# Where TensorE's operands start in a partition: one byte modulo 256 for all of them, in an attention and Fourier-mixing kernel

## The chip, the cores and the metric

The kernel runs on one core of a Trainium2 chip. The metric is the device time of one execution in microseconds (us), the median of several runs. TensorE (PE) multiplies matrices: an LDWEIGHTS loads a 128x128 stationary operand from the on-chip memory, and the MATMUL behind it streams a moving operand of up to 512 columns past it. VectorE (DVE), ScalarE (ACT) and GpSimd (POOL) work on tiles; SyncE (SP) issues most of the transfers.

## The reference, cut to what matters

Four layers on x of 2048 rows and 640 numbers, each with a residual sum and a layer norm without gains ahead of it.

```python
x = x + A(layernorm(x)); x = x + B(layernorm(x))
x = x + A(layernorm(x)); x = x + B(layernorm(x))

A: q, k, v = x @ wqkv                     # 32 heads of 20 numbers
   row s sees rows s, s-2, ..., s-14      # 8 taps, masked at the start
   o = softmax(q.k * scale) @ v;  return o @ wo
B: a = x @ dft_hid_re.T;  b = x @ dft_hid_im.T
   return dft_seq_re @ a - dft_seq_im @ b
```

## The kernel before, in words

**Products.** Every float32 number that TensorE multiplies is held as a pair, a rounded high part (float32r) and the low rest. A product is three passes, high by high, high by low, low by high (`PASSES`).

**Layer A** (`layer_a`, layers 0 and 2) is written as a list of steps, ordered by hand into phases; nothing reorders the engines' queues afterwards. The rows stand in 4 chunks c of 4 groups j of 128 rows. For each chunk, each quarter q of the weights and each j, `qkv_mm` (L366) makes one product of 15 matmuls: stationary is the transposed x of the group, in the buffer `s{j}`, moving are 480 columns of a weight row k of `wq[q]`, in the buffer `r1_{q}`. ACT empties the result (`qkv_evac`, L373), transfers put q, k and v into DRAM and fetch windows of them into the five buffers `win`. DVE multiplies (L435, L475) and reduces (L445), POOL adds (L438, L494, L495), and `wo_mm` (L519) makes the output product. The transposes go through TensorE as well (L331, with the corrections of L339).

**Layer B** (`LayerB`, layers 1 and 3). `z_mm` and `zpart` (L982) make the first of eight column tiles of the sequence transform in layer A's tail (t = 0), and the second one after it (t = 1): 16 slices s by 15 matmuls each, stationary `xn[c]` with c = s // 4, moving the split coefficients in the buffer that `c_tag` names. For t = 0 it is s2, s3, s0 in turn (s1 for the last), for t = 1 s3 and s0 in turn. The other six tiles are made two at a time by `pair`, three times in a layer, with seven products where the plain way has eight; each is called `product` (L1161). A pair has three sections of eight steps i, 432 matmuls of 512 columns in all. `ymm` (L1064) is the transform along the 640 numbers, matmuls of 320 columns.

The normalized x of chunk c, `xn[c]`, lies in the buffer `r1_{c}`, the same that held the weights of quarter q = c. `product` takes its stationary operand from there in two ways: `x_plain` reads chunk c where it lies; `x_slot` fetches a precombined block into a place of `xn[c]`, going around a ring of such places: c = 0 (four places), then c = 1 (four places). The steps of a pair's second section stand in this order:

```python
self.product(m2, x2, p11, *ends)                            # banks xt, t0; x2, x1: the ring
self.product(f1, self.x_plain(*k1(i), 512), p11, i == 0, False)  # bank pq; chunk 0 for i < 4
self.product(f2, self.x_plain(*k2(i), 512), p22, i == 0, False)  # bank t1; chunk 2 or 3
self.product(m1, x1, c1, *ends)                             # banks m0, m1
self.product(f1, self.x_plain(*k2(i), 512), p21, False, i == NP - 1)  # bank pq
```

Two ring places are used in each step of this section, so its steps 0, 1, 4 and 5 read chunk 0, the steps 2, 3, 6 and 7 chunk 1.

**Where buffers lie.** A tile is asked for by a tag, `T(shape, tag)`. Each tag has one place (or `bufs` places) in every partition, as large as the largest tile that bears it. The places follow each other in the order in which the tags are first asked for, so the start of each one is the sum of the sizes ahead of it. The starts of the tags that matter, as bytes in a partition and modulo 256:

| buffer | start before | modulo 256 | start after | modulo 256 |
|---|---|---|---|---|
| ident, nident | 16544, 17056 | 160 | 16544, 17056 | 160 |
| s3 | 17568 | 160 | 17600 | 192 |
| r1_0 | 22784 | 0 | 22720 | 192 |
| pr0 | 43264 | 0 | 43200 | 192 |
| win (five) | 48384 and on | 0, 192, 128, 64, 0 | 48320 and on | 192, 128, 64, 0, 192 |
| pr1, pr2, pr3, r1_1, r2a, r1_2, r1_3, zo2, zo3, ot, s0, s1, stg, s2, zo0, zo1, xa | 65984 and on | 192 | the same | 192 |

Parts of a tile that TensorE reads start 512, 1024, 1280, 2048, 2560 or 10240 bytes apart, all multiples of 256, with one exception: a weight row of `wq[q]` has 480 numbers, 1920 bytes, which is 7.5 times 256. So the moving operands of L366 begin at 0 and 128 in turn for q = 0, and at 192 and 64 in turn for q = 1, 2, 3.

Of the kernel before, what the change touches and what calls it, by code (L numbers as in the profile page):

```python
# [11 lines left out]
F32R = mybir.dt.float32r  # L12
# [8 lines left out]
D = 640  # L21
# [5 lines left out]
P = 128  # L27
# [2 lines left out]
NQ = 4  # L30
KD = D // P
F = 160
HQ = 8
NE = 8
FE = 80
# [20 lines left out]
NWIN = 5  # L56
# [16 lines left out]
SLOTS = NJ + W - 1  # L73
# [5 lines left out]
def tile_layers(ctx: ExitStack, tc: tile.TileContext, x, wqkv, wo, cs, wre, wim, out):  # L79
# [10 lines left out]
    def nm(base):  # L90
        uid[0] += 1
        return f"{base}_{uid[0]}"

    def T(shape, tag, dt=F32, bufs=1, pool=None):
        return (pool or sb).tile(shape, dt, tag=tag, name=nm(tag), bufs=bufs)

    def pt(shape, tag, bufs=1):
        return ps.tile(shape, F32, tag=tag, name=nm(tag), bufs=bufs)
# [5 lines left out]
    make_identity(nc, ident)  # L104
    nident = T([P, P], "nident", F32R)
    nc.scalar.activation(nident, ident, AF.Copy, scale=-1.0)
    zero = T([P, D], "s3", mybir.dt.bfloat16)
    nc.vector.memset(zero, 0.0)
    wb = pt([P, 512], "m1")
    for i in range(NWARM):  # L110
        nc.tensor.matmul(wb, zero[:, :P], zero[:, :512], start=True, stop=True)
    mhalf = T([P, 4], "mhalf")
    nc.gpsimd.memset(mhalf, -0.5)
    mask = T([P, SLOTS], "mask")
    nc.gpsimd.memset(mask, 0.0)
    nc.gpsimd.memset(mask[0:2, 0:3], NEG)
    nc.gpsimd.memset(mask[0:1, 3:7], NEG)
# [11 lines left out]
    def split(hi, lo, src, neg=False, eng=None):  # L129
        nc.scalar.activation(hi, src, AF.Copy, scale=-1.0 if neg else 1.0)  # L130
        if neg:
            nc.vector.scalar_tensor_tensor(lo, src, -1.0, hi.bitcast(F32), op0=ALU.mult, op1=ALU.subtract)
        else:
            (eng or nc.vector).tensor_tensor(lo, src, hi.bitcast(F32), op=ALU.subtract)
# [68 lines left out]
    def wtile(shape):  # L203
        return T(shape, "win", bufs=NWIN)

    def wq_load(q, k0, k1, tag):
        raw = T([P, k1 - k0, 3 * F], tag)
        nc.sync.dma_start(raw, wqkv[q][:, k0:k1, :])
        return raw

    def wq_load1(q, k):
        raw = wtile([P, 3 * F])
        nc.sync.dma_start(raw, wqkv[q][:, k, :])
        return raw

    def a_weights_q(q):
        wt = T([P, 2, KD, 3 * F], f"r1_{q}", F32R)
        for k in range(KD):
            split(wt[:, 0, k], wt[:, 1, k], wq_load1(q, k))
        return wt  # L220
# [25 lines left out]
    def layer_a(li, stats, handoff, prev):  # L246
# [4 lines left out]
        wq = {}  # L251
# [6 lines left out]
        win = {}  # L258
# [97 lines left out]
        def qkv_mm(g, cqj):  # L356
# [4 lines left out]
            for a, b in PASSES:  # L361
                for k in range(KD):
                    if n == (10 if g < 2 else 5):
                        for fn, args in mid.pop(g, ()):
                            fn(*args)
                    nc.tensor.matmul(mt[g][:, : 3 * F], st[:, a, k], wq[q][:, b, k], start=n == 0, stop=n == 14)  # L366
                    n += 1

        def qkv_evac(g, cqj):
            c, q, j = cqj  # L370
            if j % 2 == 0:
                sgs[q] = T([P, 6, 2, FE], "stg", bufs=2)
            nc.scalar.copy(sgs[q][:, :, j % 2], mt.pop(g)[:, : 3 * F].rearrange("p (a f) -> p a f", f=FE))  # L373

# [167 lines left out]
            nstats[c].finish(j0, j1)  # L542

        def wq_begin(q):
            wq[q] = T([P, 2, KD, 3 * F], f"r1_{q}", F32R)

        def wq_raw(q):
            if q < 3:
# [15 lines left out]
        def wq_late(q, k):  # L564
            if k == 0:
                wq_begin(q)
            wq[(q, k)] = wq_load1(q, k)
# [23 lines left out]
        def early():  # L591
# [4 lines left out]
            def w0():  # L596
                with tc.issue_after(prev.dma.ins):
                    wq[0] = a_weights_q(0)
# [32 lines left out]

        def prologue_first():
            wq_begin(0)
            for j, (k0, k1) in enumerate(((0, 3), (3, 5))):
                x_load(0, j, f"pr{j}")
# [4 lines left out]
            for q in (1, 2, 3):  # L640
                wq_begin(q)
                wq_raw(q)
# [753 lines left out]
```

## Time and profile before

| | |
|---|---|
| median of 3 runs | 1762.35 us (1760.95 to 1767.62) |
| profiled execution, first to last instruction (span) | 1757.1 us |
| what lies around the span, against the fastest run | about 3.9 us |
| granted TensorE clock | 0.999 of full speed |
| busy: PE, DVE, ACT, POOL | 1731.3, 1375.7, 807.6, 621.2 us |

The execution that was profiled has no time of its own outside the profile; its span is the one to set against the runs, and is 5.2 us below their median. The first layer A runs from the start to about 390 us, the first layer B until 860, the second layer A until about 1253, and the second layer B to the end.

A matmul's duration in the profile (its last column leaves later than the next matmul begins) is longer than the time that it holds the engine. What counts for the sum is the time from one start to the next, called a slot below. The timeline view puts runs of equal instructions into one row: start, duration, the group, and the number xN; the starts of two following rows, divided by N, give the slot. In the chain of waits, pieces of TensorE go from start to start, so a piece divided by its N is a slot as well. The names of the operands in a row stand without their numbers: r is any of `r1_0` to `r1_3`, s any of `s0` to `s3`, and the two inputs are sorted by name, not by role.

### The profile page before, as it was taken

To read this page: it belongs to the slowest core of one execution; us is meant where nothing else is said; L and a number is where in the kernel's file an instruction comes from. 1 tells how busy PE (TensorE), PEld (TensorE's weight loads), DVE (VectorE), ACT (ScalarE), POOL (GpSimd) and SP (SyncE) were. 2 spreads that over 40 slices of the span, in tenths; PEclk is the share of its full clock that TensorE was granted. 3 is DMA by queue.
4 is the path that set the end of the run, shared out by engine and by line. 5 is a ranking of instruction groups with operands and counts; after the bars stand their busy time and mean duration, and the time that the engine had idled before them with its cause. 6 is when DMAs were issued, how large, how long until landed. Compare 5 with 4: busy or idle time off the path is not lost.

```text
span 1757.1 us, 26454 instructions
## 1 busy us (share of the span) xinstructions
PE 1731.3 (99%) x8798; PEld 1501.6 (85%) x8798; DVE 1375.7 (78%) x2131; ACT 807.6 (46%) x1682; POOL 621.2 (35%) x585
## 2 busy tenths in 40 slices
PE   9999999989999999999999999989999999999999
PEld 7889897868888888888998899978788888888888
DVE  6999999988667767767648999989887677677673
ACT  4664544554445445445534434444434443443441
POOL 4799998940000000000028998889200000000000
PEclk9999999999999999999999999999999999999999
DMA  8996769759777777787657866798687767767761
GB/s 286 311 325 207 225 200 334 264 174 306 257 262 249 244 254 239 235 272 227 195 178 235 269 205 211 223 328 279 205 313 260 253 197 261 256 208 237 262 202 53
DMA packets 273961, 426.20 MB, mean 243 GB/s; under 512 B 22656, under 2 KB 153728, under 8 KB 273568
## 3 DMA queue, kind: packets, MB, share of 16 engines
q1 hardware_dynamic: 270624, 422.54, 72.7%
q10 hardware_dynamic: 3200, 1.97, 0.4%
q8 instruction: 70, 1.15, 0.3%
q14 instruction: 67, 0.55, 0.1%
HBM read 339.28 MB, written 85.14 MB: 242 GB/s over the span
## 4 chain that ended last, share of the span: by engine, by line
PE 83%; DVE 7%; DMA 4%; POOL 3%; issue 2%; ACT 1%; SPq 0%; DVEq 0%; ACTq 0%; POOLq 0%
PE m L366 20%; PE aux L1064 16%; PE t L1161 11%; PE m L1161 11%; PE pq L1161 6%; PE xt L1161 6%; PE aux L519 4%; PE t L982 3%; PE m L982 3%; DVE pr L475 2%; DMA win<-kvb 2%; PE xt L982 2%; DVE pr L435 1%; DVE lg L445 1%; POOL pr L494 1%
## 5 line engine op out<-in xcount | busy, mean ns | idle before, releaser
L366 PE MATMUL m<-r,s 128*128 128x480 f32 x1920 | 436.2, 381 | 0.7 <-DVE r L649 0.2
L366 PEld LDWEIGHTS m<-r,s 128*128 128x128 f32 x1920 | 355.5, 188 | 54.4 <-DVE r L649 1.0
L1064 PE MATMUL aux<-r2a,zo 128*128 128x320 f32 x768 | 226.6, 310 | 0.0
L1154 ACT CAST r<-win 128x512 fp32r<-128x512 f32 x246 | 149.9, 620 | 163.2 <-DVE win L1190 84.7
L494 POOL TENSOR_TENSOR pr<-pr 128x640 f32<-128x640 f32 x126 | 205.8, 1633 | 33.2 <-DVE pr L475 33.0
L1064 PE MATMUL aux<-pr,zo 128*128 128x320 f32 x704 | 208.3, 308 | 0.0
L178 POOL TENSOR_TENSOR stats<-stats,mhalf 128x1 f32<-128x1 f32 (+1 forms) x40 | 29.5, 737 | 493.4 <-ACT stats L174 484.5
L1155 DVE TENSOR_TENSOR r<-win,r 128x512 fp32r<-128x512 f32 x246 | 165.7, 688 | 45.2 <-ACT r L1154 44.1
L435 DVE TENSOR_TENSOR pr<-pq,win 128x1280 f32<-128x1280 f32 x128 | 189.8, 1483 | 13.9 <-DMA win<-kvb 8.0
L475 DVE TENSOR_TENSOR pr<-pq,win 128x1280 f32<-128x1280 f32 x128 | 190.7, 1491 | 5.1
L438 POOL TENSOR_TENSOR pr<-pr 128x640 f32<-128x640 f32 x116 | 166.3, 1434 | 16.6 <-DVE pr L435 13.6
L1161 PE MATMUL m<-r,r 128*128 128x512 f32 x594 | 152.6, 392 | 0.0
L1064 PEld LDWEIGHTS aux<-r2a,zo 128*128 128x128 f32 x768 | 144.1, 188 | 2.0
L1161 PE MATMUL t<-r,r 128*128 128x512 f32 x498 | 135.0, 392 | 0.0
L1064 PEld LDWEIGHTS aux<-pr,zo 128*128 128x128 f32 x704 | 132.2, 188 | 2.1
L1161 PEld LDWEIGHTS m<-r,r 128*128 128x128 f32 x594 | 111.4, 188 | 24.7
L982 PE MATMUL m<-s,r 128*128 128x512 f32 x384 | 118.8, 396 | 7.7 <-DMA s<-c0b 4.9
L445 DVE TENSOR_REDUCE lg<-pr 128x64 f32<-128x640 f32 (+1 forms) x128 | 112.1, 876 | 7.1 <-POOL pr L438 6.8
L982 PE MATMUL t<-s,r 128*128 128x512 f32 x384 | 117.5, 393 | 0.2 <-DVE ot L1039 0.2
L495 POOL TENSOR_TENSOR pr<-pr 128x320 f32<-128x320 f32 x126 | 112.0, 889 | 9.9
L1161 PEld LDWEIGHTS t<-r,r 128*128 128x128 f32 x498 | 93.5, 188 | 21.4
L373 ACT COPY stg<-m 128x480 f32<-128x480 f32 x128 | 70.9, 555 | 82.0 <-PE m L366 61.8
(299 smaller groups left out, 3206.0 us busy)
## 6 DMA issues: line engine op xcount, KB each, us to landing
win<-cs_in SPq DMA_DIRECT2D x351, 256.0 KB, 3.8
r<-xc SPq DMA_DIRECT2D x240, 256.0 KB, 4.1
win<-kvb SPq DMA_DIRECT2D x96, 440.0 KB, 4.4
xa<-cs_in SPq DMA_DIRECT2D x121, 256.0 KB, 3.8
win<-kvb SPq DMA_DIRECT2D x64, 360.0 KB, 4.7
kvb<-stg SPq DMA_DIRECT2D x60, 320.0 KB, 4.6
xc<-stg SPq DMA_DIRECT2D x32, 512.0 KB, 4.4
s<-c0b SPq DMA_DIRECT2D x26, 512.0 KB, 6.1
```

What stands on the lines that cost most here:

```text
L366: nc.tensor.matmul(mt[g][:, : 3 * F], st[:, a, k], wq[q][:, b, k], start=n == 0, stop=n == 14)
L435: nc.vector.tensor_tensor(pr, q, wview(u, jp, 0, [[1, FE]]), op=ALU.mult)
L438: nc.gpsimd.tensor_tensor(pv[:, :, 0:10], pv[:, :, 0:10], pv[:, :, 10:20], op=ALU.add)
L445: nc.vector.tensor_reduce(lgs[u][:, :, 2 * jp : 2 * jp + 2].rearrange("p h j w -> p (j w) h"), prq.pop((u, jp)), axis=AX.X, op=ALU.add,)
L475: nc.vector.tensor_tensor(pr.rearrange("p j w (h d) -> p j w h d", d=DH), lgs[u][:, :, 2 * jp : 2 * jp + 2].rearrange("p h j w -> p j w h" ...
L494: g.tensor_tensor(pr[:, :, 0:4], pr[:, :, 0:4], pr[:, :, 4:8], op=ALU.add)
L495: g.tensor_tensor(pr[:, :, 0:2], pr[:, :, 0:2], pr[:, :, 2:4], op=ALU.add)
L982: self.last = nc.tensor.matmul(self.z[t][k], self.xn[c][:, a, j, k * P : (k + 1) * P], self.ct[s][:, b], start=s == 0 and i == 0, stop=s = ...
L1064: self.last = nc.tensor.matmul(self.ym[e][:, :320], zt[(k, a, ri)][:, j2 * P : (j2 + 1) * P], w[:, e * 320 : (e + 1) * 320], start=(k, a, ...
L1154: nc.scalar.copy(hi, raw)
L1155: nc.vector.tensor_tensor(lo, raw, hi.bitcast(F32), op=ALU.subtract)
L1161: nc.tensor.matmul(bank, w(a, kb), hl[b], start=start and (a, b) == (0, 0), stop=stop and (a, b) == (1, 0),)
```

## The change

Two things are changed. The tags are asked for in another order at the start: `mhalf` comes ahead of s3, and r1_0, pr0 and `win` are asked for ahead of `mask` by tiles that nothing uses, so s3, r1_0 and pr0 begin at 192 modulo 256 like the others. And the tile of the split weights has rows of 512 numbers, of which 480 are used, so that each row of `wq[q]` begins at 192 as well; the buffers `r1_{q}` do not grow by it, since `xn[c]` needs as much. Every engine has the same instructions in the same order, of the same shapes, as before; only addresses differ.

```diff
+QPAD = 512
...
     nc.scalar.activation(nident, ident, AF.Copy, scale=-1.0)
+    mhalf = T([P, 4], "mhalf")
     zero = T([P, D], "s3", mybir.dt.bfloat16)
+    for tag, w in (("r1_0", D), ("pr0", D), ("win", SLOTS * FE)):
+        T([P, w], tag, bufs=NWIN if tag == "win" else 1)
+    mask = T([P, SLOTS], "mask")
     nc.vector.memset(zero, 0.0)
     wb = pt([P, 512], "m1")
     for i in range(NWARM):
         nc.tensor.matmul(wb, zero[:, :P], zero[:, :512], start=True, stop=True)
-    mhalf = T([P, 4], "mhalf")
     nc.gpsimd.memset(mhalf, -0.5)
-    mask = T([P, SLOTS], "mask")
     nc.gpsimd.memset(mask, 0.0)
...
     def a_weights_q(q):
-        wt = T([P, 2, KD, 3 * F], f"r1_{q}", F32R)
+        wt = T([P, 2, KD, QPAD], f"r1_{q}", F32R)[:, :, :, : 3 * F]
...
         def wq_begin(q):
-            wq[q] = T([P, 2, KD, 3 * F], f"r1_{q}", F32R)
+            wq[q] = T([P, 2, KD, QPAD], f"r1_{q}", F32R)[:, :, :, : 3 * F]
```

## The prediction

> **What bounds the kernel now.** I read the page first, then the stretches of the span, the waits of DVE, the chain of waits, and last the timeline of single groups of matmuls.
>
> ```profile
> span 1757.1 us, 26454 instructions
> PE 1731.3 (99%) x8798; PEld 1501.6 (85%) x8798; DVE 1375.7 (78%) x2131; ACT 807.6 (46%) x1682; POOL 621.2 (35%) x585
> PEclk9999999999999999999999999999999999999999
> PE 83%; DVE 7%; DMA 4%; POOL 3%; issue 2%; ACT 1%; SPq 0%; DVEq 0%; ACTq 0%; POOLq 0%
> L366 PE MATMUL m<-r,s 128*128 128x480 f32 x1920 | 436.2, 381 | 0.7 <-DVE r L649 0.2 <-DVE r L646 0.2
> ```
>
> TensorE has work for 99% of the span at an unthrottled clock, and makes 83% of the chain that ended last. But an average over stages can mislead, so I look at stretches (columns: stretch, length, busy PE, PEld, DVE, ACT, POOL, clock, transfer share, GB/s).
>
> ```profile
> 100.00:150.00 50.00, 50.00 (x252) 43.74 (x251) 47.88 (x63) 29.97 (x72) 48.00 (x44) 1.00 0.88 290
> 200.00:250.00 50.00, 50.00 (x270) 45.23 (x269) 47.63 (x74) 21.94 (x56) 46.60 (x45) 1.00 0.66 203
> 350.00:400.00 50.00, 43.65 (x202) 35.48 (x202) 41.91 (x66) 26.88 (x57) 19.93 (x21) 0.97 0.53 174
> 600.00:700.00 100.00, 100.00 (x479) 84.79 (x478) 71.19 (x116) 48.18 (x91) 1.74 (x2) 1.00 0.76 251
> 1150.00:1200.00 50.00, 44.97 (x243) 39.12 (x242) 43.34 (x68) 23.09 (x61) 44.56 (x43) 1.00 0.97 343
> 1600.00:1700.00 100.00, 100.00 (x487) 85.36 (x486) 72.97 (x120) 44.87 (x77) 0.00 (x0) 1.00 0.73 240
> ```
>
> In layer B (600 to 700, 1600 to 1700) PE is full and DVE has a quarter of its time free, so PE alone is the bound. In layer A (100 to 250) PE and DVE are both full, DVE at 47.6 to 47.9 of 50 us; the rest is the few hundredths of a us between its instructions, since its waits from 45 to 245 us come to only 3.4 us in 6 places, 5 of them on POOL:
>
> ```profile
> DVE lg L445 <- POOL pr L438: 2.7, 5, 1.1
> DVE pr L435 <- ACT pq L408: 0.7, 1, 0.7
> ```
>
> At layer A's end (350 to 400, 1150 to 1200) PE has gaps. So a faster PE shortens layer B one for one, and in layer A only what comes before DVE is full. The chain of waits (start, length, what) agrees on where PE hands over:
>
> ```profile
> 19.52 34.70 PE m L366 x160
> 271.14 7.79 DMA win<-kvb
> 631.35 8.82 PE aux L1064 x60
> 904.20 25.97 PE m L366 x120
> 959.72 22.85 PE m L366 x105
> 1155.36 7.68 DMA s<-c0b
> ```
>
> **What the change does to one matmul.** No instruction is added, removed or moved; every term is the slot of a matmul whose operands start at another byte. The trace already holds both kinds. First the second section of a pair in layer B (timeline of PE: start, duration, group):
>
> ```profile
> 647.68 1.56 PE L1161 MATMUL m<-s,r 128*128 128x512 f32 x6
> 649.08 0.86 PE L1161 MATMUL pq<-s,r 128*128 128x512 f32 x3
> 649.77 0.85 PE L1161 MATMUL xt<-r,r 128*128 128x512 f32 x3
> ...
> 652.54 1.52 PE L1161 MATMUL m<-r,r 128*128 128x512 f32 x6
> 653.90 0.84 PE L1161 MATMUL pq<-r,r 128*128 128x512 f32 x3
> 654.58 0.84 PE L1161 MATMUL xt<-s,r 128*128 128x512 f32 x3
> 655.26 0.84 PE L1161 MATMUL t<-s,r 128*128 128x512 f32 x3
> 655.94 0.86 PE L1161 MATMUL pq<-s,r 128*128 128x512 f32 x3
> 656.64 0.85 PE L1161 MATMUL t<-s,r 128*128 128x512 f32 x3
> ```
>
> The row at 647.68 is m1 of step 1, whose weights come from chunk 0, r1_0, byte 0, against moving operands at 192: 649.08 - 647.68 = 1.40 us for 6, a slot of 233.3 ns. The row at 652.54 is the same product in step 2 with chunk 1, r1_1, all at 192: 1.36 us for 6, 226.7 ns. Step 3 shows it within two us: xt and t read r1_1, 0.68 us for 3 (226.7); pq at 655.94 is f1 with chunk 0 again, 0.70 for 3 (233.3). So unequal bytes cost 6.6 ns a matmul. And the row at 649.08, all at 192 but right behind unequal ones, takes 0.69 for 3: 230.0, half of the price lingers.
>
> The other unequal buffer, s3 as moving operand at 160, in L982 (five products go to m, m, xt, t, t, so two m rows are five slots apart):
>
> ```profile
> 434.36 0.63 PE L982 MATMUL m<-s,r 128*128 128x512 f32 x2
> 435.53 0.63 PE L982 MATMUL m<-s,r 128*128 128x512 f32 x2
> ...
> 437.83 0.61 PE L982 MATMUL m<-s,r 128*128 128x512 f32 x2
> 438.97 0.39 PE L982 MATMUL m<-s,r 128*128 128x512 f32 x1
> ```
>
> With s3: 1.17 / 5 = 234.0 ns. With s0 at 192, one slice later: 1.14 / 5 = 228.0. Two different bytes (0 and 160), one in the weights and one in the stream, cost the same; that makes the inequality the likely cause and not one bad address.
>
> For L366 no row shows 480 columns with all operands at 192, so its slot is bounded. Now it is 34.70 / 160 = 216.9, 25.97 / 120 = 216.4 and 22.85 / 105 = 217.6 ns, of mixed bytes. L1064, whose operands lie at 192 nearly everywhere, has 8.82 / 60 = 147.0 for 320 columns; with 226.7 for 512 that is 79.7 / 192 = 0.415 ns a column, so 480 equal columns should take 226.7 - 32 x 0.415 = 213.4: a gain of 3.6 on 217. The other end is a loss: the 6.6 ns on top of 213.4, 220.0, 3.0 more than now. I take the gain, since both shapes at hand follow the line.
>
> **The sum, part by part.**
> - L1161, 6 pairs of 432 matmuls. From the code a pair has 144 with r1_0: 48 each in ring places of the first and second section, and 48 by `x_plain` of chunk 0 (12 in the second, 36 in the third). 864 x 6.6 ns = 5.7 us, all in layer B where PE is the bound. Of the 1728 equal ones I estimate that half stand close behind unequal ones and carry the 3.3 ns of the row at 649.08: 864 x 3.3 = 2.9 us.
> - L982, t = 1, where PE is the bound: ten of sixteen slices have s3 or chunk 0, 150 x 2 layers x 6.6 = 2.0 us. For t = 0, in layer A's tail, eight of sixteen: 240 x 6.6 = 1.6 us, half of it counted, 0.8, since PE has gaps there.
> - L366: the matmuls ahead of DVE's full time, about 165 at the start (until 50 us) and 250 of the second layer A (860 to 945): 415 x 3.6 = 1.5 us. The other 1505, 5.4 us, fall where DVE is full; a PE that is done earlier waits there, and I count a fifth, 1.1 us, for DVE's waits that hang on PE through ACT.
> - The rest is nothing or near it. L1064 with pr0 (byte 0) is a tenth of its matmuls, and L519 has its operands at 192 already. The transposes keep ident at 160. DVE's and ACT's instructions see other bytes in `win`, r1_0 and pr0. That is costed at nothing because L435 already reads `win` at bytes 0, 64, 128 and 192 and writes pr0 (0) or a buffer at 192, and hardly differs (ns min/median/max):
>
> ```profile
> L435 DVE TENSOR_TENSOR pr<-pq,win x128: 1474/1484/1494, 33.1 to 1223.7; 128x1280 f32<-128x1280 f32 x128
> ```
>
> If that were wrong, it would count at once, for DVE covers nothing in layer A: 10 ns on each of these 128 would be 1.3 us. Transfers into s3, r1_0 and `win` land at other bytes; in layer B PE's fullness shows them hidden, in layer A's tail they are on the chain (7.79 and 7.68 us), with no row that tells one byte from another, and I leave them as they are, either sign.
>
> Sum: 5.7 + 2.9 + 2.0 + 0.8 + 1.5 + 1.1 = 14.0 us. The transposes and the pauses will still leave some matmuls behind unequal ones; I take a tenth off: 12.5 us. The span goes from 1757.1 to 1744.6, and the median from 1762.35 to about **1750**. The low end of the gain is the unequal ones alone in PE's stretches, 5.7 + 2.0 = 7.7, 1754.6 us. The high end is every term in full with nothing swallowed, 5.7 + 2.9 + 3.6 + 6.9 = 19.1, 1743 us. DVE, a quarter free in layer B, stays behind PE there: what is late next is only the transfers, which would have to lose the slack that one per cent takes.
>
> **The rivals.**
> *The byte is not the cause (no change, 1762).* The three odd buffers are also the three lowest large ones in the partition (17568, 22784, 43264), and they stay there; if the place, or the chunk's order in the work, made the 6.6 ns, the rows stay as they are. Against it: two of these buffers in two roles with one price, and L366, which with buffers high up (r1_1 to r1_3, rows in turn at 192 and 64) is above the line of the equal ones too. The Trainium skill speaks for this rival: "TensorE: Matmul & The Clock Gate", section "Step-by-step: what each phase is for", gives TensorE two independent read ports, so that loading the next weights takes nothing from the running stream, and by that no relation between the two addresses could matter. The rows at 652.54 and 647.68, 226.7 against 233.3 ns, do not agree with that as it stands. Chance 0.14.
>
> *The padding breaks a good run.* Before, a weight row begins at the byte modulo 256 where the row ahead of it ended; padded, each begins 128 bytes beyond. Should that matter, L366 goes to the 220.0 of the upper bound: 1920 x 3.0 = 5.8 us more, all of it felt, because PE has no gap from 100 to 250 us. Then 5.7 + 2.9 + 2.0 + 0.8 - 5.8 = 5.6 us are gained, 1756.7. For it: 480 columns are no whole number of 256 bytes, the other two shapes are. Chance 0.10.
>
> *Equal bytes collide (slower).* If the weight load and the stream starting at one byte met at the same place at each matmul, and the present 226.7 came only from the unequal neighbours that shift them apart, all of L1161 and L982 would go to 233.3 and L366 to 220.0. The equal L1161 would lose 864 x 6.6 + 864 x 3.3 = 8.6 us, the equal L982 of t = 1 180 x 6.6 = 1.2, L366 5.8: 15.6 us slower, 1778. It decides as soon as long runs without any unequal matmul are slower than those at 652.54. Against it: from 652.54 to 655.94 fifteen equal ones in a row stay at 226.7, and grow no slower with distance from the last unequal one. Chance 0.08.
>
> **How the numbers follow.** My forecast has 0.68, with its own range 1743 to 1754.6. The range should leave out 0.2: it goes from 1743 up through the padding rival to 1760, which leaves out the slower rival and most of the no-change one. About 0.5%, 8.8 us, is what a measurement of this kernel can tell from nothing, as its runs differ by 6.7 us. Faster by more means under 1753.5: nearly all of my forecast, and a little of the padding rival, 0.67. Within it: the forecast's weak end, most of the padding rival and no change, 0.26. Slower: 0.07.
>
> **What would show it.** Right: the m rows of L1161 at 226.7 in every step, with no 233.3; L982 with s3 at 227; chain pieces of L366 at 213 to 214 a matmul; layer B shorter by some 5 us each time; DVE's stretches in layer A unchanged, and PE's gaps before 400 us longer by 2 to 3 us. Wrong: 233.3 still in the rows that read r1_0 (no cause), L366 near 220 (padding), 226.7 gone everywhere (collision), or layer A longer by more than 2 us, which would mean a transfer or DVE that minds the byte.

## The result, and the profile after

The changed kernel takes 1756.82 us (median of 8 runs, 1750.60 to 1760.61) where the kernel before, run beside it, takes 1763.45 (8 runs, 1760.32 to 1767.62). The ratio is 0.9957, with a 95% interval from 0.9945 to 0.9968: a gain of 7.6 us, 5.6 to 9.7. The forecast was 12.5 us, to 1750. The sign, the mechanism and the main term hold; two of the smaller terms do not, and a part of the main one does not arrive in the time.

The two profiled executions hardly differ in span, 1757.1 and 1755.8 us. That is chance: a run's time is its span plus 1.8 us (not the 3.9 that was set down for the kernel before), and by that the profile of before was of a quicker execution than all 8 runs beside it. Other executions of both kernels were profiled for this reason (below).

The page of after, with the same lines as before:

```profile
span 1755.8 us, 26454 instructions
PE 1725.6 (98%) x8798; PEld 1501.8 (86%) x8798; DVE 1374.0 (78%) x2131; ACT 805.0 (46%) x1682; POOL 621.2 (35%) x585
PE 75%; DVE 11%; DMA 7%; POOL 3%; issue 3%; ACT 1%; SPq 0%; DVEq 0%; ACTq 0%; POOLq 0%
L369 PE MATMUL m<-r,s 128*128 128x480 f32 x1920 | 435.8, 381 | 1.2 <-DVE r L649 0.5
```

(Lines stand 3 further down than before: L366 is L369, L982 is L985, L1161 is L1164.) PE is busy for 5.7 us less, and its share of the chain that ended last falls from 83% to 75%, while DVE's rises from 7% to 11% and that of the transfers from 4% to 7%. What PE gave up is partly handed to others. And the row of L369 is what it was: 381 ns, 435.8 us in all.

Stretches of layer A and of its two tails (same columns as in the prediction):

```profile
100.00:150.00 50.00, 50.00 (x251) 43.75 (x250) 47.89 (x63) 29.97 (x72) 47.99 (x44) 1.00 0.89 291
350.00:400.00 50.00, 44.90 (x204) 36.60 (x203) 42.24 (x67) 26.95 (x57) 20.30 (x21) 0.93 0.54 175
1150.00:1200.00 50.00, 46.21 (x242) 40.42 (x243) 43.14 (x68) 22.35 (x58) 44.40 (x43) 0.97 0.98 343
```

DVE has the same instructions in the same time (47.89 us x63 against 47.88 x63). In the last two rows PE's clock is 0.93 and 0.97, where it was 0.97 and 1.00; the last section comes back to that.

The chain of waits has the pieces of L366 and L1064 again:

```profile
631.31 8.79 PE aux L1067 x60
903.52 26.02 PE m L369 x120
959.08 22.80 PE m L369 x105
```

8.79 / 60 = 146.5 ns for 320 columns. For 480 columns 26.02 / 120 = 216.8 and 22.80 / 105 = 217.1, where 213.4 was forecast and 216.4 to 217.6 stood before. The timeline of PE in the second section of the same pair, all rows now at one byte:

```profile
647.44 1.52 PE L1164 MATMUL m<-s,r 128*128 128x512 f32 x6
648.80 0.84 PE L1164 MATMUL pq<-s,r 128*128 128x512 f32 x3
649.48 0.84 PE L1164 MATMUL xt<-r,r 128*128 128x512 f32 x3
...
655.60 0.84 PE L1164 MATMUL pq<-s,r 128*128 128x512 f32 x3
656.28 0.84 PE L1164 MATMUL t<-s,r 128*128 128x512 f32 x3
```

m1 of step 1, from chunk 0, takes 648.80 - 647.44 = 1.36 us for 6, 226.7 ns, where it took 1.40; pq right behind it 0.68 for 3, where it took 0.69; f1 of chunk 0 at 655.60 0.68, where it took 0.70. All are 226.7 now: the unequal price is gone, and so is the 3.3 ns that lingered behind it.

L982 behind the first layer A, t = 1 (the m rows, five slots apart):

```profile
427.20 0.62 PE L985 MATMUL m<-s,r 128*128 128x512 f32 x2
428.33 0.61 PE L985 MATMUL m<-s,r 128*128 128x512 f32 x2
429.46 0.62 PE L985 MATMUL m<-s,r 128*128 128x512 f32 x2
430.78 0.74 PE L985 MATMUL m<-s,r 128*128 128x512 f32 x2
432.07 0.62 PE L985 MATMUL m<-s,r 128*128 128x512 f32 x2
```

The first two steps read s3 and take 1.13 / 5 = 226.0 ns, where such steps took 234.0: the price of s3 is gone as well. But then steps of 1.32 and 1.29 us follow. The waits of the stretch 385 to 465 us tell what they are; the first row is of PE's weight loads, the second of DVE:

```profile
PEld m L985 <- DVE s L972: 1.5, 4, 0.4
...
DVE stg L1124 <- DMA xc<-stg: 8.0, 5, 2.7
```

The row of L972, the split of a slice's coefficients on DVE, has no counterpart among PE's waits of that stretch in the first profile of before, and 0.9 us in the second (below); the second of after has 1.5 us again, order only 2.1. DVE's own wait is an old one; before it reads:

```profile
DVE stg L1121 <- DMA xc<-stg: 8.2, 5, 2.5
```

DVE stands there until transfers into `xc` have emptied the two `stg` buffers of `x_combine`, and the splits are queued behind it. It comes no earlier than before, so a PE that is quicker waits longer.

**Where the time went.** From the starts of all matmuls I took every slot and subtracted 0.4167 ns x columns + 13.3 ns, the line through 320 and 512 equal columns. What is over by less than 60 ns is summed as excess, what is over by more as pauses (these include slots at a lowered clock). Beside it stand the lengths of four stretches by the start of the first and the last matmul of `product` in each layer B:

| profile | excess L1161 / L982 / L366 | pauses | to first B's pairs | pairs | to second B's pairs | pairs | span |
|---|---|---|---|---|---|---|---|
| before | 8.9 / 4.0 / 7.5 | 44.1 | 463.1 | 394.6 | 474.2 | 393.4 | 1757.1 |
| before, again | 8.8 / 4.0 / 7.4 | 48.1 | 464.1 | 396.5 | 474.7 | 393.7 | 1760.9 |
| after | 1.3 / 1.4 / 7.3 | 54.0 | 463.1 | 394.0 | 475.6 | 391.2 | 1755.8 |
| after, again | 1.3 / 1.3 / 7.3 | 49.3 | 464.0 | 393.2 | 472.5 | 389.9 | 1751.4 |
| order only | 1.3 / 1.2 / 5.8 | 54.6 | 464.7 | 393.3 | 475.6 | 389.6 | 1755.1 |
| padding only | 8.9 / 4.0 / 8.5 | 53.1 | 464.6 | 397.4 | 477.1 | 396.1 | 1767.0 |

L1161 sheds 7.6 us and L982 2.6 to 2.7. Of that the mean of the three profiles with equal bytes against the two of before arrives in the pairs (2.0 and 3.3 us) and not ahead of them (463.9 against 463.6, 474.6 against 474.5). The pauses are 1 to 10 us longer. Part of that is the clock: each spell of 3.41 us at half the clock (last section) puts 1.7 us into them, and the traces have, in the order of the table, 1, 0, 3, 1, 2 and 2 such spells ahead of the last matmul. Without them the pauses are 42.4, 48.1, 48.9, 47.6, 51.2 and 49.7 us. So the profiles with equal bytes wait some 4 us longer than the two of before on average, but padding only, with the old bytes, waits as long as they do: where the missing part goes is less sure than that it is missing.

### The profile page after: what moved, and what is told of

Read it like the earlier page. It is cut to its first block, busy times and chain, and to the rows that moved or that the text cites. A ratio compares the mean times of both kernels' runs of the same rounds, so it can differ in the third digit from the quotient of the medians.

```text
span 1755.8 us, 26454 instructions
## 1 busy us (share of the span) xinstructions
PE 1725.6 (98%) x8798; PEld 1501.8 (86%) x8798; DVE 1374.0 (78%) x2131; ACT 805.0 (46%) x1682; POOL 621.2 (35%) x585
## 4 chain that ended last, share of the span: by engine, by line
PE 75%; DVE 11%; DMA 7%; POOL 3%; issue 3%; ACT 1%; SPq 0%; DVEq 0%; ACTq 0%; POOLq 0%
PE m L369 21%; PE aux L1067 13%; PE t L1164 10%; PE m L1164 9%; PE pq L1164 5%; PE xt L1164 5%; PE aux L522 4%; DMA win<-cs_in 3%; PE m L985 2%; PE t L985 2%; DVE pr L478 2%; DVE pr L438 1%; PE xt L985 1%; POOL pr L497 1%; DMA win<-kvb 1%
## 5 line engine op out<-in xcount | busy, mean ns | idle before, releaser
L369 PE MATMUL m<-r,s 128*128 128x480 f32 x1920 | 435.8, 381 | 1.2 <-DVE r L649 0.5
L369 PEld LDWEIGHTS m<-r,s 128*128 128x128 f32 x1920 | 355.1, 188 | 54.9 <-DVE r L652 1.0
L1158 DVE TENSOR_TENSOR r<-win,r 128x512 fp32r<-128x512 f32 x246 | 165.4, 687 | 42.8 <-ACT r L1157 41.6
L1164 PE MATMUL m<-r,r 128*128 128x512 f32 x594 | 151.0, 389 | 0.0
L1164 PE MATMUL t<-r,r 128*128 128x512 f32 x498 | 133.8, 390 | 1.0 <-DVE r L1158 1.0
L1164 PEld LDWEIGHTS m<-r,r 128*128 128x128 f32 x594 | 111.3, 188 | 22.9
L985 PE MATMUL m<-s,r 128*128 128x512 f32 x384 | 119.5, 399 | 7.5 <-DMA s<-c0b 3.4
L985 PE MATMUL t<-s,r 128*128 128x512 f32 x384 | 117.8, 394 | 0.2 <-DVE ot L1042 0.2
L1164 PEld LDWEIGHTS t<-r,r 128*128 128x128 f32 x498 | 93.4, 188 | 21.4 <-DVE r L1158 1.4
```

Of the source, the lines that this page charges most:

```text
L985: self.last = nc.tensor.matmul(self.z[t][k], self.xn[c][:, a, j, k * P : (k + 1) * P], self.ct[s][:, b], start=s == 0 and i == 0, stop=s = ...
L1158: nc.vector.tensor_tensor(lo, raw, hi.bitcast(F32), op=ALU.subtract)
L1164: nc.tensor.matmul(bank, w(a, kb), hl[b], start=start and (a, b) == (0, 0), stop=stop and (a, b) == (1, 0),)
```

## The experiments

**1. One half of the change at a time.** The tags in the new order, the rows of 480 numbers as before (against after):

```diff
-QPAD = 512
+QPAD = 480
```

> Only the order of the tags is changed (s3, r1_0, pr0 at byte 192); weight rows of L366's product stay at 480 numbers. Theory (the relation of the bytes, and the tags alone): slots of layer B's product 226.7 ns throughout, L366's product at 216 to 217 ns a matmul, ratio to before 0.994 to 0.997, as the whole change. Rival (the padding earns part of it): 0.997 to 0.999, and slower than the whole change by 2 us or more.

Measured: 1757.43 us (12 runs), ratio 0.9973 (0.9958 to 0.9988). The other half, the padded rows with the tags in the old order (against before; the same edit in `wq_begin`):

```diff
+QPAD = 512
-        wt = T([P, 2, KD, 3 * F], f"r1_{q}", F32R)
+        wt = T([P, 2, KD, QPAD], f"r1_{q}", F32R)[:, :, :, : 3 * F]
```

> Only the weight rows are padded to 512 numbers; s3 stays at byte 160, r1_0 and pr0 at 0. Theory (padding does nothing by itself): ratio to before 0.9985 to 1.0015, layer B's matmuls with chunk 0 at 233.3 ns, L366's product at 216 to 218 ns. Rival (padding has a price or gain of its own): over 1.002 or under 0.998.

Measured: 1763.92 us (12 runs), ratio 1.0010 (0.9995 to 1.0025). The whole change, run once more beside these:

> The changed kernel once more, beside the others. Theory: ratio to before 0.9945 to 0.997; slots of layer B's product at 226.7 ns, but PE waits of some 5 us in layer B for splits and transfers, at other places than in the first profile. Rival (those waits belong to the first profile alone): the profile's span is 1750 us or less.

Measured: 1753.89 us (8 runs), ratio 0.9964 (0.9949 to 0.9978), so the gain is there again. In its profile PE's waits in `product` come to 2.6 us, half of what was expected. The order of the tags by itself makes most of the gain, and the padding by itself none. Whether the padding adds something to the order the times do not settle: order only was 3.5 us slower than the whole change (medians), as the rival has it, but the two intervals overlap from 0.9958 to 0.9978. The slots show nothing that it could add. The chains of waits, order only and then padding only:

```profile
904.82 25.93 PE m L369 x120
960.24 22.76 PE m L369 x105
```

```profile
908.51 26.09 PE m L367 x120
964.21 22.89 PE m L367 x105
```

216.1 and 216.8 ns with rows in turn at 192 and 64, 217.4 and 218.0 padded in the old places, and 216.8 and 217.1 in after with all at one byte. They lie within 2 ns of each other, none is near 213.4, and the padded ones are the slower ones.

All 1920 slots together show a small price of the byte after all. I gave each matmul of L366 the bytes that the code gives its two operands, and left out slots with a pause. Over the line lie equal ones by 3.6 to 4.0 ns (in before, order only and after), rows 128 bytes apart by 2.3 to 2.6 (before and order only), and the others, which are 32, 64 or 96 apart modulo 128 where buffer s3 or r1_0 takes part, by 5.2 (before). So inequality, which costs 6.6 ns at 512 columns, costs about 1.3 ns at 480, and the padding, which made the rows 128 apart equal, took back what the new order gave: the excess of L366 is 7.5 us before, 5.8 in order only and 7.3 in after.

**2. More unequal bytes.** The kernel before, with tags asked for early so that s3, r1_0 and pr0 lie at 160, pr1 to pr3 and r1_1 at 96 and the rest at 192; now chunk 1 is unequal too, and higher up in the partition:

```diff
+    for tag, w in (("r1_0", D), ("pr0", D), ("win", SLOTS * FE), ("pr1", D), ("pr2", D), ("pr3", D), ("r1_1", D)):
+        T([P, w], tag, bufs=NWIN if tag == "win" else 1)
     mhalf = T([P, 4], "mhalf")
+    mask = T([P, SLOTS], "mask")
     nc.gpsimd.memset(mhalf, -0.5)
-    mask = T([P, SLOTS], "mask")
     nc.gpsimd.memset(mask, 0.0)
```

> The two small tags mhalf and mask are asked for only behind r1_1, so that s3, r1_0 and pr0 start at byte 160, pr1 to pr3 and r1_1 at 96, and the rest at 192: 2016 of the 2592 matmuls of layer B's product have unequal bytes, where before has 864. Theory (inequality costs 6.6 ns a matmul, wherever the buffers lie): 1152 x 6.6 = 7.6 us more, less the 2.9 us that the equal ones behind unequal ones carry already: 5 us slower than before, ratio 1.002 to 1.005; slots of 233 ns also with chunk 1. Rival (the low place of s3 and r1_0 is what costs): these stay where they were within 96 bytes and nothing else goes low, so ratio 0.999 to 1.001 and chunk 1 at 226.7 ns.

Measured: 1768.35 us (5 runs), ratio 1.0049 (1.0034 to 1.0064): 6.0 to 11.3 us slower than before. Its timeline of PE in the same section:

```profile
650.59 1.56 PE L1163 MATMUL m<-s,r 128*128 128x512 f32 x6
651.99 0.86 PE L1163 MATMUL pq<-s,r 128*128 128x512 f32 x3
...
655.47 1.56 PE L1163 MATMUL m<-r,r 128*128 128x512 f32 x6
656.87 0.86 PE L1163 MATMUL pq<-r,r 128*128 128x512 f32 x3
```

The row at 655.47 is the m1 of chunk 1 that took 1.36 us; it takes 1.40, as chunk 0 does at 650.59, and its pq takes 0.70 where it took 0.68. The excess of L1161 goes from 8.9 to 15.7 us, and the pairs last 400.7 and 397.2 us. A buffer that had been equal, high up in the partition, gets the price of 6.6 ns as soon as its byte differs (96 against 192). The rival of the low place falls, and so does that of colliding equal bytes, since the kernel with the fewest equal bytes is the slowest of before, after and this one.

One more rival is left: that 192 is the only good byte, for each operand by itself. The same trace speaks against it, since s3 and r1_0 both lie at 160 here and meet in L982 (t = 1, m rows five slots apart):

```profile
394.31 0.63 PE L984 MATMUL m<-s,r 128*128 128x512 f32 x2
395.48 0.63 PE L984 MATMUL m<-s,r 128*128 128x512 f32 x2
...
397.80 0.62 PE L984 MATMUL m<-s,r 128*128 128x512 f32 x2
398.94 0.61 PE L984 MATMUL m<-s,r 128*128 128x512 f32 x2
400.07 0.63 PE L984 MATMUL m<-s,r 128*128 128x512 f32 x2
```

With s0 at 192 against r1_0 at 160 a step takes 1.17 us, 234.0 ns a slot; one slice later, with s3 at 160 against r1_0 at 160, 1.14 and 1.13 us, 228.0 and 226.0 ns. In the kernel before, s3 at 160 against r1_0 at 0 took 234. So it is the relation of the two bytes that counts. But 6.6 ns is not the price of every unequal pair: s3 at 160 against r1_1 at 96 takes 229 to 230 ns in this trace (slices 4, 6 and 7), half of it.

**3. Where the shortfall is.** First one more look at the kernel before:

> The kernel before, profiled once more. Its first profile had a span of 1757.1 us, under every time of its runs less the 1.8 us that lie around a span. Theory (the first profile was a lucky one in its waits): span 1759 to 1765 us, the same slots, and some us more of PE waits in layer B. Rival: 1757 us again.

Measured: 1762.64 us, span 1760.9, with the same excess as the first (the table); the first profile of before was a quick execution by chance. Then the waits of after that the first profile of before lacks (PE's waits over the whole span):

```profile
PE xt L1164 <- DVE r L1158: 1.6, 2, 1.0
PE t L1164 <- DVE r L1158: 1.0, 1, 1.0
PE xt L1164 <- DVE s L1158: 0.9, 1, 0.9
```

In the first profile of before, the like of them is one row:

```profile
PE xt L1161 <- DVE r L1155: 0.3, 1, 0.3
```

In the second profiles the two kernels do not differ in them, 1.4 us in before and 1.3 in after, so these rows alone show nothing new in after. L1158 splits the coefficients of `product`, whose raw tiles are fetched on the same queue as the ring of `x_slot`. So the fetches into the ring were left out, in before and in after:

```diff
-            nc.sync.dma_start(v.bitcast(F32), self.xc[m][:, i])
```

> The kernel before, without the 240 transfers that fetch precombined blocks into the ring of layer B's product (the product reads what lies there, so its result is another; TensorE's work is the same). Theory (the changed kernel loses part of its gain to waits for layer B's transfers): this one is 2 to 6 us faster than before (ratio 0.9965 to 0.999), its PE slots unchanged. Rival (transfers cost layer B nothing): 0.999 to 1.001.

> The changed kernel, without the same 240 transfers. Theory: with the transfers relieved the slots' full 10 to 11 us of layer B come through: 10 to 12 us faster than the kernel before without them, ratio between the two 0.993 to 0.9945. Rival (the missing part of the gain is lost elsewhere): the two differ by 6 to 8 us, as they do with the transfers.

Measured: 1760.35 us (ratio 0.9979, 0.9969 to 0.9990) and 1752.55 (0.9940, 0.9924 to 0.9955). The two differ by 7.8 us, no more than the full kernels, as the rival has it. But the profiles show the pairs as the theory wanted them: 393.7 and 393.1 us before, 389.6 and 389.1 after, together 8.1 us shorter, the whole excess of L1161 and a little over. What came out there was lost ahead of the first pairs, which begin at 467.8 us against 464.7, with 18.9 us of pauses in L982 against 12.9; some 1.7 us of it is a spell at half the clock. So the fetches do hold up the pairs, and the stage of L982 is a second place where time goes.

For that place the stores into `xc`, for which DVE waits in `x_combine`, were left out as well, besides the fetches:

```diff
-            if apart:
-                for h, v in enumerate((hi, lo)):
-                    nc.sync.dma_start(self.xc[m][:, i : i + 2, h], v.bitcast(F32))
-            else:
-                nc.sync.dma_start(self.xc[m][:, i : i + 2], hl.bitcast(F32))
```

> The kernel before, without the 240 fetches into the ring and also without the 56 transfers that store the precombined blocks (L1121 to L1123 still compute them; nothing reads them, so the result is another). Theory (in layer B's first stage, t = 1, DVE waits some 8 us a layer for buffers that these stores hold, and the splits for L982 queue behind it): faster than without the fetches alone by 1 to 4 us, ratio to before 0.995 to 0.998. Rival (the stage is bound by something else): as without the fetches alone, 0.998.

> The changed kernel with the same fetches and stores left out. Theory: what L982 gains in its slots at t = 1 (2 us) now comes through beside layer B's pairs (8 us): 9.5 to 11 us faster than the kernel before without them, ratio between the two 0.9938 to 0.9946. Rival (L982's gain is lost elsewhere): 7 to 8 us, as without the fetches alone.

Measured: 1756.94 us (ratio 0.9958, 0.9943 to 0.9974) and 1747.11 (0.9898, 0.9879 to 0.9918). The two differ by 9.8 us. In after without fetches and stores, PE's waits for DVE's L972 are gone from the stretch 385 to 465; the longest of its weight loads there is

```profile
PEld xt L985 <- DVE zo L1042: 0.8, 1, 0.8
```

and between the two kernels the excess of L982 falls from 3.9 to 1.0 us, with 9.0 us of pauses in L982 instead of 11.5. The pairs are 4.3 and 4.0 us shorter. With neither fetch nor store the equal bytes come through in nearly full size: 7.7 + 2.9 us of excess less, 9.8 us of time. With both in place 7.6 us arrive. By the spread of these runs the 9.8 are good to about 1.5 us and the 7.6 to about 2, so the traces show that the waits go away, and that the time follows is likely, but not clear of chance.

Could the wait be removed without leaving work out? `XAPART` names the pairs of precombined blocks that use other buffers than `stg`; here more of them do (against order only):

```diff
-XAPART = {(m, i) for i in range(2, NP - 2, 2) for m in (7, 1)}
+XAPART = {(m, i) for i in range(0, NP - 2, 2) for m in (7, 1)}
```

> The tags in the new order, no padding, and in layer B's first stage the blocks 7 and 1 of the first step too go through the buffers xa instead of stg. Theory (stg's stores hold up DVE there, and PE behind it): PE's pauses in L982 shrink by 1 to 4 us, ratio to before 0.993 to 0.996. Rival (xa is taken by the hidden-dimension weights at that time): DVE waits there instead, 0.996 to 0.999.

Measured: 1767.88 us (12 runs), ratio 1.0022 (1.0010 to 1.0034), slower than before. Its waits over the whole span:

```profile
DVE xa L1124 <- DMA xc<-xa: 9.9, 5, 3.5
PE m L985 <- DVE s L972: 5.7, 8, 1.5
```

The wait moves from `stg` to `xa`, and PE's wait for the splits behind it, 2.1 us in order only, grows to 5.7 us. No version with all its work beats after beyond the noise.

**4. What 480 columns cost.** If the byte does not lift L366 above the line, its width might. (In the next two runs all operands lie at 192.) In after, 14 of the 15 matmuls of each product got 448, 464, 416 and 384 columns for q = 0 to 3:

```diff
-                    nc.tensor.matmul(mt[g][:, : 3 * F], st[:, a, k], wq[q][:, b, k], start=n == 0, stop=n == 14)
+                    w = 3 * F if n == 0 else (448, 464, 416, 384)[q]
+                    nc.tensor.matmul(mt[g][:, :w], st[:, a, k], wq[q][:, b, k, :w], start=n == 0, stop=n == 14)
```

> The changed kernel, with L366's product cut short: 14 of its 15 matmuls stream 448 columns for q = 0, 464 for q = 1, 416 for q = 2, 384 for q = 3 (the rest of the columns is left out). What a slot has above the line through 320 and 512 equal columns (columns x 0.4167 + 13.3 ns) is 4 ns at 480. Theory (a stream that is no whole number of 256 bytes misses the good case): 448 and 384, which are, take 200.0 and 173.3 ns; 464 and 416 take 207 to 214 and 187 to 194, above the line. Rival (layer A's other work costs every stream 4 ns): all four are 4 ns above the line, 204.0, 210.7, 190.7, 177.3.

Measured: one run, 1750.34 us, span 1748.5. The groups of L370 by shape:

```profile
L370 PE MATMUL m<-r,s 128*128 128x464 f32 x448 | 99.1, 372 | 0.0
L370 PE MATMUL m<-r,s 128*128 128x416 f32 x448 | 89.3, 350 | 0.0
L370 PE MATMUL m<-r,s 128*128 128x384 f32 x448 | 84.4, 338 | 0.0
L370 PE MATMUL m<-r,s 128*128 128x448 f32 x448 | 98.6, 368 | 1.8 <-ACT s L357 1.1 <-DVE r L650 0.3 <-DVE r L653 0.3
```

A mean here is the slot plus 162 ns (389 stands where slots are 226.7). By the line 384, 416, 448 and 464 columns should read 335.3, 348.6, 362.0 and 368.6: they are 2.7, 1.4, 6.0 and 3.4 above it. These means hold pauses too; the slots without a pause are about 1, 1, 4 and 3 ns above the line. 448 columns, which are a whole number of 256 bytes, are not free of it, and 416, which are not, nearly are. That is neither of the two expected patterns.

Since each width had its own buffer there, the widths were dealt out anew, other ones in each layer A (the padding is set to zero and read where w is over 480):

```diff
...
+                    w = 3 * F if n == 0 and first else ((384, 416, 464, 448) if first else (512, 320, 496, 352))[q] if n else 512
...
```

> The changed kernel, with L366's product at other widths for 14 of its 15 matmuls: in the first layer A 384, 416, 464, 448 columns for q = 0 to 3, in the second 512, 320, 496, 352 (the padding is cleared, and read by the wide ones; other columns are left out). Theory (the excess over the line hangs on the width): 1 ns at 384 and 416, 3 to 4 at 448 and 464 as in the first sweep although they now stand in other buffers, about 0 at 512 and 320. Rival (it hangs on the buffer or the place in the order): 3 to 4 ns for q = 0 and 1, 1 for q = 2 and 3, whatever the width; 512 and 320 then 4 ns above the line in layer A.

Measured: one run, 1743.33 us, span 1741.4. Four of its groups:

```profile
L372 PE MATMUL m<-r,s 128*128 128x496 f32 x224 | 54.7, 397 | 0.0
L372 PE MATMUL m<-r,s 128*128 128x448 f32 x224 | 49.6, 373 | 0.0
L372 PE MATMUL m<-r,s 128*128 128x416 f32 x224 | 44.6, 350 | 0.0
L372 PE MATMUL m<-r,s 128*128 128x320 f32 x224 | 35.4, 309 | 0.0
```

320 columns are on the line (309 against 308.6), 416 again barely above it, 448 again well above it although it is now another buffer's, and 496 (397 against 382.0, pauses included) as well. In the slots without a pause the excess is 0.0 ns at 320, about 1 from 352 to 416, 3 to 4 from 448 to 496, and at 512 the median is 1.3. So most of it is the width; why these widths, the runs do not tell.

`widths` tells one thing more. It takes 14 / 15 x 52 columns on average x 0.4167 ns x 1920 = 39 us of PE's work out of L366. The time is 13.8 us below that of before beside it, where after gains 7.6, so some 6 us of the 39 are felt. In its first layer A the pairs of B begin at 463.8 us as ever; the stretch to the second B's pairs is 467.6 us instead of 472.5 to 475.6. A PE with less to do waits more, and its clock is at half for 20.5 us in this run, which takes another 10 us. Even with these, the greater part of the 39 us was never on the path: L366 does not set the end of layer A alone.

## Why the prediction was right, and where it was wrong

- **The number.** 1756.82 us is 7 us from the forecast, and outside the forecast's own range of 1743 to 1754.6. It lies in the wider range only because that was drawn up to 1760 for the padding rival. That it meets this rival's 1756.7 is luck: padding alone is excluded as the reason (experiment 1).
- **The unequal price (right).** 6.6 ns a matmul in L1161 and L982, read from four rows of the profile before, is what went away (226.7 and 226.0 ns in after), and what comes when a third buffer is made unequal. The Trainium skill, "TensorE: Matmul & The Clock Gate", section "Step-by-step: what each phase is for", states two independent read ports, by which the weight load takes nothing from the running stream. From that one would expect no relation of the two addresses to matter, and these rows do not agree; the measurement decides.
- **The terms of L1161, 5.7 + 2.9 = 8.6 us.** In slots 7.6, a little less, which is about the tenth taken off. The step that failed is "what is late next is only the transfers, which would have to lose the slack": by the runs without the fetches they did lose it. With them 5.3 us arrive in the pairs, without them 8.1. That it is by way of the splits, whose raw tiles share a queue with the ring, is likely but not shown: PE's waits for them are 3.5 and 1.3 us in the two profiles of after, 0.3 and 1.4 in those of before.
- **The terms of L982, 2.0 + 0.8 = 2.8 us.** In slots 2.6 to 2.7, but nothing arrives. "L982, t = 1, where PE is the bound" is wrong: DVE's splits, queued behind its wait for the stores, are just ahead of PE there, and the gain turns into pauses (in L982 9.7 and 11.2 us before, 15.0 and 12.1 in after). Without fetches and stores the pair of kernels differs by 9.8 us.
- **The terms of L366, 1.5 + 1.1 = 2.6 us, were nothing (wrong).** The slot of 480 columns was put on the line between 320 and 512; the two bounds, 213.4 and 220.0, held the 216.9 that it stayed at, but the value taken was the lower one. The profile before held the answer, though in no row of the views: some 500 of its matmuls in L366 have both operands at 192, and taken one by one they stand 3.6 to 3.9 ns above the line, near 217. Most of the excess hangs on the width: equal bytes leave 480 columns 3.6 to 4.0 ns above the line, and the price of unequal ones, 6.6 ns at 512 columns, is about 1.3 ns here. And had the slot fallen, little of it would have been felt: 39 us out of L366 brought some 6.
- **The padding rival** (L366 at 220.0) did not come either: padding alone is 1.0010 (0.9995 to 1.0025), not 5.8 us.
- **The checks.** The m rows and s3 came as named. Layer B shorter by "some 5 us each" came out as 2.0 and 3.3. DVE's stretches in layer A are unchanged, as named. PE's gaps before 400 us, named as 2 to 3 us longer, are not: 14.0 and 15.8 us in the profiles of before, 13.8 and 15.0 in those of after.

In sum: 14.0 forecast in terms, of which 2.6 (L366) never existed, 10.2 to 10.3 were freed in slots, and 5.6 to 9.7 are measured. The runs without fetches and stores point to waits behind DVE and the transfers for the rest; in single profiles these waits vary by as much as is missing.

## What to carry to other kernels

Read one product in two buffers from the timeline: start-to-start times of equal matmuls tell a price of 3% that no busy share shows. Here the starts of the stationary and the moving operand had to agree: at 512 columns differences of 32, 64 and 96 bytes modulo 128 cost 6.6 ns in most pairs and 3 in one, at 480 columns about 1.3. A difference of 128 costs nothing at 480; at 512 no run has one. When an engine that is 99% busy gets 0.6% faster, look for who is less than that ahead of it: about a quarter of this gain did not arrive (10.3 us freed, 7.6 measured), and leaving out transfers for which DVE waits brought most of it back. A slot of another width has to be measured; neither its length nor the price of a byte can be carried over.

## What the hardware showed that was not expected

**The width.** For these float32r pairs 448 to 496 columns cost 3 to 4 ns more than the line on which 320 and 512 lie. 512 columns take 226.7 ns. The Trainium skill, "TensorE: Matmul & The Clock Gate", section "Back-to-back issue gap", gives N / 2.4 + 2.5 ns for an isolated matmul, which makes 215.8 at 512 columns (an estimate by that formula), and about 131 ns for a stream of weight loads and matmuls. The first fits other matmuls of this kernel: the 18 in bf16 at its start (L111), 512 columns with a weight load each, stand 215 to 217 ns apart once the clock is full. The other 11 ns come with float32r, or with something else in which the two differ; no run tells. Nothing here is near 131.

**A pause of 1.9 us can cost 1.7 us more.** The timeline of PE in the kernel with more blocks in `xa` (x3 rows, so slots of 413 and 427 ns), and its granted clock in steps of 2 us (the third number from the end):

```profile
472.85 1.44 PE L1164 MATMUL t<-r 128*128 128x512 f32 x3 [1.93 <-DVE ot L1047]
474.09 1.48 PE L1164 MATMUL t<-r,r 128*128 128x512 f32 x3
475.37 1.36 PE L1164 MATMUL pq<-r,r 128*128 128x512 f32 x3
```

```profile
472.00:474.00 2.00, 1.15 (x3) 0.97 (x4) 1.53 (x4) 1.59 (x4) 0.00 (x0) 0.76 0.39 141
474.00:476.00 2.00, 2.00 (x6) 1.52 (x5) 1.77 (x3) 1.18 (x4) 0.00 (x0) 0.50 0.55 158
476.00:478.00 2.00, 2.00 (x9) 1.60 (x9) 0.58 (x1) 0.62 (x1) 0.00 (x0) 0.88 0.57 164
```

After 1.93 us of waiting the clock is at half for some 3.4 us, which costs (0.24 + 0.50 + 0.12) x 2 = 1.7 us. The same pause does not always do it. In both profiles of before PE waits 1.92 us for POOL near 370 us; then the same 12 matmuls take, in the first and in the second,

```profile
370.74 3.55 PE L519 MATMUL aux<-r2a,zo 128*128 128x320 f32 x12 [0.48 <-ACT zo L335]
```

```profile
371.85 2.37 PE L519 MATMUL aux<-r2a,zo 128*128 128x320 f32 x12 [0.47 <-ACT zo L335]
```

One such spell is 0.001 of the span, and the runs of one kernel go by it: of 62 runs of before, those with a mean granted clock of 1.000 have a mean of 1760.7 us (8 runs), 0.999 1761.5 (19), 0.998 1763.0 (23), 0.997 1766.1 (8); four more lie lower in the clock, at 1766.4 and 1768.0. These runs are of three chips, with medians of 1760.8, 1763.9 and 1764.2 us, and part of it may be the chip; on the one with 25 runs the means go from 1759.3 us (1.000, 5 runs) to 1764.7 (0.997, 4). That is read from the runs, and was not tested by an experiment. It does not explain the gain, since before and after have the same mean clock (0.9983 and 0.9984 over 62 and 16 runs).
